# Moving one attention unit's tail tiles and six small matmul trios in a fused attention and mixture-of-experts kernel

## The chip, the cores and the metric

The kernel runs on one core of a Trainium2 chip. A core has five engines with their own instruction queues: PE (TensorE, matmuls, with PEld as its weight loads), DVE (VectorE), ACT (ScalarE), POOL (GpSimd) and SP (SyncE, used here to issue DMAs). Each engine works through its own queue in program order and waits on semaphores that other engines and DMAs raise. The metric is the device time of one execution in microseconds (us); less is better.

## The reference, cut to what matters

Three stages follow each other. The first is causal attention over 4 batches, 8 heads, 576 tokens and 64 dimensions with a decay bias from `s`; the second is a mixture-of-experts layer whose input is the attention output, the third a gated convolution layer.

```
scores = scale * q @ k.T                          # per batch and head
cum = cumsum(maximum(s, 0))
scores = where(causal, -1e9, scores + minimum(-(cum_i - cum_j), 0))
attn = softmax(scores)
x = attn @ v                                      # 576 x 64 per head
...
x = moe(x, w_gate, w_local, w1, w2)               # one expert per token
out = conv_gate(x, w_in, conv_w, w_out)
```

The change touches only the beginning of the attention stage.

## The kernel before

The attention works in 8 units of 4 heads (unit `u` is half of a batch). A unit has 14 score tiles, `(head, g)`, each a tile of 512 columns: `g` 0 and 1 are a head's own key blocks, `g` 2 is shared by two heads, and on odd heads `g` 2 and `g` 3 are the tails, the last 64 of the 576 tokens. One score tile is one step of the loop over `t` at the end of `attention`. At step `t`, PE makes the scores of tile `t` (`scores`, L482, L485, L510); ACT takes the exponentials of tile `t-1` (`weights`, L521, L526, L527); DVE forms the low half of tile `t-2` (`rest`, L538); and four steps after the last tile of a head PE multiplies with v (`values`, L554).

A unit needs work ahead of its first step. `load` brings k and q from memory (L166, issued by SP), `split_hi` on ACT (L259) and `split_lo` on DVE or POOL (L265 to L268) cut them into two f16 halves, `turn` transposes them by DMA (L277, SP), `extra` adds the decay rows (L281), and `copy` on DVE (L285) puts them in place. `stage_a` makes scores only for their row maxima, in 14 pieces (PE L382, DVE L385 and L413); `max_turn` (PE L450), `max_out` (ACT L455) and `max_row` (DMA L462, L465) bring the maxima into row 70 of the operands. `loadv` loads v of half a batch (L176, L180: twelve DMAs), and `split_v` cuts it (ACT L342 and DVE L346 for unit 0, POOL L344 to L350 for the others).

When each of these is issued is written in the table `PAR` by step number: `PAR["start"]` for unit 0 and the preparation of units 1 and 2 (negative numbers stand before step 0; within a step, in the order of the fraction), `PAR["u1"]`, `PAR["u2"]`, `PAR["u3"]` and `PAR["u"]` for the later units, relative to the first step of the unit (step 14 for unit 1). `pa` and `pn` are the first step and the number of steps of the 14 pieces, `sv` the step of `split_v`, `mx` the step of the maxima. `BEGIN` holds the order of unit 0's tiles; index 1 is used. All engines' queues follow from the order in which this code runs.

`busy(z, n)` issues `n` products of a unit matrix, 512 columns wide, into a PSUM tile that nobody reads (L368).

The pool `zps` has three PSUM tiles for scores; a score tile gives its place back when its exponentials (or, for a tile with a low half, the subtraction on DVE) are done. `mps` has one tile, which `busy` and `max_turn` share. `aps` has two for the pieces.

Of the kernel before, what the change touches and what calls it, by code (L numbers as in the profile page):

```python
# [42 lines left out]
class Keep:  # L43
# [3 lines left out]

PAR = {'u1': {'sv': -6, 'pa': -6, 'pn': 4, 'mx': -3},  # L50
 'u2': {'at': (-22, -21, -19, -18.9, -18), 'cp': (-14, -13), 'lv': -11, 'sv': -2, 'pa': -12, 'pn': 7, 'mx': -6},
 'u3': {'load': -35, 'loadq': 0, 'at': (-33, -30, -28, -27, -26.9), 'cp': (-22, -21), 'sv': -1, 'pa': -20, 'pn': 14, 'mx': -6},
 'u': {'load': -51,
# [34 lines left out]
           'hk1': -17,  # L88
           'mob': -16,
           'mrb': -15,  # L90
           'tlk': -14,
           'tlq': -13,
           'lk1': -12,
           'xt': -11,
           'T1k': -10,
           'ttk': 2.0,
           'ttq': 3.0,
           'hq1': 3.05,
           'lq1': 3.06,
           'T1q': 3.07,  # L100
           'x1': 3.08,
           'lk2': 3.09,
           'lq2': 3.095,
           'ct': 4.0,
           'pt': 4.1,
           'c2': 4.5,
           'mtt': 5.0,
           'mot': 5.1,
           'mrt': 5.2,
           'sv0': 5.4,  # L110
           'z': 6.0,
           'lv1': 6.1},
 'r': {'cut': 12, 'w1': 6, 'w2': 8, 'w3': 22},
 'm': 'faafaafaafaa'}


BEGIN = ([(0, 0), (0, 1), (1, 0), (1, 1), (0, 2), (1, 2), (1, 3)],
         [(0, 0), (0, 1), (1, 0), (1, 1), (2, 0), (2, 1), (0, 2), (1, 2), (1, 3), (3, 0), (3, 1), (2, 2), (3, 2), (3, 3)])


def attention(tc, ctx, q, k, v, s, xd, rt, hook):
# [46 lines left out]
    def loadv(b, part=None, D=Q):  # L168
        if part in (None, 0):
            U[b, "v"] = natv.tile([128, H, 4, 64], F32, name="nv")  # L170
            U[b, "vt"] = natv.tile([128, H // 2, 64], F32, name="nvt")
        w, wt = U[b, "v"], U[b, "vt"]
        h = slice(0, H) if part is None else slice(NH * part, NH * part + NH)
        for j in range(4):
            for t in range(2):
                D.dma_start(w[64 * t:64 * t + 64, h, j], v[b, h, 128 * j:128 * j + 128].rearrange("h (p t) d -> t p h d", t=2)[t])  # L176
        for e in range(2):
            for t in range(2):
                r = 64 * e + 32 * t
                D.dma_start(wt[r:r + 32, h.start // 2:h.stop // 2], v[b, h, 512:576].rearrange("(r e) (p t) d -> e t p r d", e=2, t=2)[e, t])  # L180
# [148 lines left out]
    def split_v(u):  # L329
        b, o = u // 2, u % 2 * NH  # L330
        a, t = U[b, "v"][:, o:o + NH], U[b, "vt"][:, o // 2:o // 2 + 2]
        w = U[u, "vv"] = vp.tile([128, NH, 4, 2, 65], F16, name="vv")
        wt = U[u, "vvt"] = vp.tile([128, NH // 2, 2, 65], F16, name="vvt")
        v0 = U[u, "v0"] = vp.tile([128, NH, 65], F32, name="v0")
        for x in (w, wt):
            i = (slice(None),) * (len(x.shape) - 2)
            G.memset(x[i + (0, slice(64, 65))], 1.0)
            G.memset(x[i + (1, slice(64, 65))], 0.0)
        G.memset(v0[:, :, 64:65], 1.0)
        for x, dh, dl in ((a, w[:, :, :, 0, 0:64], w[:, :, :, 1, 0:64]), (t, wt[:, :, 0, 0:64], wt[:, :, 1, 0:64])):  # L340
            if u == 0 or not PAR["h"]["vg"]:
                A.activation(dh, x, AF.Copy, scale=VS)  # L342
            else:
                G.tensor_scalar(dh, x, VS, 0.0, op0=ALU.mult, op1=ALU.add)  # L344
            if u == 0:
                V.scalar_tensor_tensor(dl, in0=x, scalar=VS, in1=dh, op0=ALU.mult, op1=ALU.subtract)  # L346
            else:
                G.tensor_scalar(x, x, VS, 0.0, op0=ALU.mult, op1=ALU.add)
                G.tensor_tensor(dl, x, dh, op=ALU.subtract)
        G.tensor_scalar(v0[:, :, 0:64], a[:, :, 0], VS if u == 0 else 1.0, 0.0, op0=ALU.mult, op1=ALU.add)  # L350
# [15 lines left out]
    def busy(z, n):  # L366
        for _ in range(n):
            PE.matmul(z.rearrange("p (x c) -> p x c", c=128), lhsT=id16, rhs=bc(id16[:, None], [128, 4, 128]), start=True, stop=True, skip_group_check=True)  # L368
# [282 lines left out]
    copy(0, "q")  # L651
    load_tail("q")
    load(1, "k")
    todo, pieces, copies = {}, {}, {6: [(1, "k")], 7: [(1, "q")]}

    def plan(t, f):
        todo.setdefault(math.floor(t), []).append((t, len(todo), f))
# [13 lines left out]
    def second_a(r):  # L671
# [12 lines left out]
        xt=extra_tail, ct=copy_tail, ldq1=lambda: load(1, "q"), lk2=lambda: load(2, "k"), lq2=lambda: load(2, "q"),  # L684
        T1k=lambda: [turn(1, e, slice(0, 1)) for e in range(2)], T1q=lambda: [turn(1, e, slice(1, 2)) for e in range(2)], x1=lambda: extra(1),
        pt=lambda: second_a(range(12, 15)), mtt=lambda: max_turn(0, None), mot=lambda: max_out(0, None), mrt=lambda: max_row(0, None),
        sv0=lambda: split_v(0), lv1=lambda: loadv(0, 1),
        z=lambda: Q.dma_start(xd[NT:NT + 128].rearrange("p (j c) -> p j c", c=256), bc(zero[:, None, 0:256], [128, 4, 256])))
    for n, t in PAR["start"].items():
        plan(t, begin_tasks[n])  # L690
# [31 lines left out]
    for t in range(N + 9):  # L722
        if t == N - 2 * PER - 6:
            early.close()
        for f in am:
            f()
        am = []
        work(t)
        at = lambda d: steps[t - d] if 0 <= t - d < N else None
        if at(0):  # L730
            scores(at(0))
        for u, i in pieces.get(t, ()):
            if i == 0:
                P[u] = stage_a(u)
            am.append(P[u][i]())
        if at(1):
            weights(at(1))
        if at(2):
            rest(at(2))
        for d, f in ((4, values), (5, norm), (6, xout)):  # L740
            y = at(d)
            if y and y[2] == (3 if y[1] % 2 else 2):
                f(y[0], y[1])
        y = at(7)
        if y and y[2] == 3 and y != (NU - 1, 1, 3):
            store(y[0], y[1] // 2)
        if at(8) == (NU - 1, 3, 3):
            rt.turn_last(U[NU - 1, "xh"], U[NU // 2 - 1, "xth"], 1, zps)
            put(NU - 1, range(1, 2))
        y = at(PAR["h"]["ps"])  # L750
        if y and y[1:] == (3, 3) and y[0] < NU - 1:
            put(y[0], range(2))
        if at(11) == (NU - 1, 1, 3):
            rt.turn_last(U[NU - 1, "xh"], None, 0, zps)
        if at(9) == (NU - 1, 1, 3):
            store(NU - 1, 0)
            put(NU - 1, range(1))
        y = at(PAR['h']['lg'])
        if y and y[1:] == (3, 3) and y[0] < NU - 1:
            rt.logits(y[0], mps.tile([128, 512], F32, name="mt"))  # L760
        y = at(PAR['h']['lg'] + PAR['h']['co'])
        if y and y[1:] == (3, 3) and y[0] < NU - 1:
            rt.collect(y[0])
        for f in tm:
            f()
        tm = []
        for n, (d, h) in enumerate(((10, 1), (12, 1), (10, 3), (12, 3), (14, 3))):
            y = at(d)
            if y and y[1:] == (h, 3) and y[0] < NU - 1 and (n < 4 or y[0] % 2):
                u = y[0]  # L770
                tm.append(rt.turn_tile(u, U[u, "xh"], U[u // 2, "xth"] if n == 4 else None, n, mps.tile([128, 512], F32, name="mt")))
        for x in copies.get(t, ()):
            copy(*x)
        hook(t)
# [803 lines left out]
```

## Time and profile before

| what | us |
|---|---|
| median of 3 runs | 713.57 |
| the 3 runs | 713.11, 713.57, 715.43 |
| the profiled execution, its own time | 710.43 |
| its span, first to last instruction | 708.7 |
| PE busy | 643.1 |
| DVE busy | 452.1 |
| ACT busy | 390.5 |
| POOL busy | 249.6 |

The profiled execution is one run with a hardware profile; its time lies 1.73 us above its span, the part of the run outside the first and the last instruction. Its mean granted TensorE clock is 0.942 of full speed. Attention fills the first 238 us; the change lies in the first 90 of them.

### The profile page before, as it was taken

The numbers are of one execution on the slowest core, as the hardware profiler recorded it, in microseconds if no ns is written. First come the engines' busy times: TensorE is split into PE (matmuls) and PEld (weight loads), VectorE is DVE, ScalarE is ACT, GpSimd is POOL, SyncE is SP. The second block draws the span as 40 slices with busy tenths as digits, with TensorE's granted clock in tenths as the row PEclk, the third lists the DMA queues.
The fourth block names the chain that finished last, engine by engine and source line by source line (L and its number), as shares of the span: only waits on it lengthen the run. The fifth ranks groups of instructions, "written<-read, shape, count | busy, mean of one in ns | idle before, by whom it ended". The sixth has DMA issues, their size and how long they took to land. (4 is left out here: it accounts for less than half of the span.)

```text
span 708.7 us, 15489 instructions
## 1 busy us (share of the span) xinstructions
PE 643.1 (91%) x5177; PEld 401.2 (57%) x5177; DVE 452.1 (64%) x859; ACT 390.5 (55%) x660; POOL 249.6 (35%) x356
## 2 busy tenths in 40 slices
PE   5668899899999566999998999999889999999997
PEld 2346778688888433444443444444367766665443
DVE  7874978988875699653885866753039985546000
ACT  5544667788788754743755563532049974645111
POOL 7456866654441059832344363333100000000000
PEclk9855989999999769999999999999999999999999
DMA  5767784756646445899999999963195000000111
GB/s 131 136 164 150 127 178 75 172 104 108 191 139 217 127 139 190 246 320 257 256 295 248 300 206 260 204 147 65 50 172 97 1 16 22 25 31 30 45 50 55
DMA packets 168828, 101.82 MB, mean 144 GB/s; under 512 B 119712, under 2 KB 147016, under 8 KB 168732
## 3 DMA queue, kind: packets, MB, share of 16 engines
q1 hardware_dynamic: 164744, 88.65, 52.2%
q0 software_dynamic: 3984, 11.99, 5.6%
q8 instruction: 47, 0.77, 0.5%
q14 instruction: 49, 0.40, 0.2%
q10 hardware_dynamic: 4, 0.00, 0.0%
HBM read 62.18 MB, written 15.31 MB: 109 GB/s over the span
## 5 line engine op out<-in xcount | busy, mean ns | idle before, releaser
L1188 PE MATMUL hp<-r,xt 128*128 x504 | 115.4, 387 | 7.9 <-ACT xt L1219 7.9
L1188 PE MATMUL yp<-r,ht 128*128 x504 | 112.2, 379 | 1.7 <-PEq L1295 1.7
L1386 PE MATMUL hp<-yt,wi 128*128 128x288 f16 x768 | 95.6, 286 | 2.5 <-DMA yt<-yd 2.5
L1434 PE MATMUL o<-wo,g 128*128 128x512 f16 x432 | 94.5, 379 | 0.0
L1188 PEld LDWEIGHTS <-xt 128*128 128x128 f16 x504 | 50.0, 99 | 69.3 <-ACT xt L1219 8.6
L1386 PEld LDWEIGHTS <-wi 128*128 128x128 f16 x768 | 75.1, 98 | 23.3 <-DMA yt<-yd 2.7
L1188 PEld LDWEIGHTS <-ht 128*128 128x128 f16 x504 | 48.5, 98 | 57.4 <-issue 1.8
L1144 DVE SCALAR_TENSOR_TENSOR r<-st,r 128x512 f32 (+3 forms) x80 | 70.7, 951 | 6.7 <-ACT r L1133 5.1
L1434 PEld LDWEIGHTS <-g 128*128 128x128 f16 x432 | 42.3, 98 | 49.5
L1133 ACT ACTIVATE r<-st 128x512 f32 (+3 forms) x84 | 57.1, 764 | 21.8 <-SPq L1181 16.8
L385 DVE TENSOR_REDUCE mx<-za 128x1 f32<-128x384 f32 (+4 forms) x97 | 57.0, 602 | 17.7 <-PE za L382 17.0
L1249 POOL DMA_INDIRECT yd<-ys,idx x21 | 23.6, 1122 | 125.6 <-DVEq L1172 77.6
L526 ACT ACTIVATE phi<-z,lnes 128x512 f16<-128x512 f32 (+1 forms) x80 | 50.6, 633 | 25.9 <-PE z L485 25.6
L482 PE MATMUL z<-k 71*128 71x128 f16 (+2 forms) x320 | 53.6, 294 | 8.5 <-ACT p L521 3.2
L538 DVE TENSOR_TENSOR plo<-z,phi 128x512 f16<-128x512 f32 (+1 forms) x80 | 48.2, 603 | 12.3 <-ACT z L527 11.7
L1403 DVE SCALAR_TENSOR_TENSOR c<-hb,cw,c 128x576 f32<-128x576 f32 x32 | 26.1, 816 | 35.3 <-ACT c L1397 35.3
L527 ACT ACTIVATE z<-z,lnes 128x512 f32<-128x512 f32 (+1 forms) x80 | 48.6, 607 | 0.0
L554 PE MATMUL o<-v,p 128*128 128x65 f32 x256 | 46.1, 293 | 0.0
L1437 ACT ACTIVATE s<-o 128x512 f32<-128x512 f32 x18 | 10.7, 597 | 63.1 <-PE o L1434 63.1
L1247 ACT ACTIVATE ys<-yp,pp 128x512 f16<-128x512 f32 x21 | 14.4, 685 | 53.5 <-PE yp L1188 32.3
L554 PE MATMUL o<-vv,phi 128*128 128x65 f16 (+1 forms) x512 | 42.7, 204 | 0.0
L554 PEld LDWEIGHTS <-phi 128*128 128x128 f16 x544 | 42.1, 110 | 0.0
(285 smaller groups left out, 1193.5 us busy)
## 6 DMA issues: line engine op xcount, KB each, us to landing
st<-in_moe_w_dram SPq DMA_DIRECT2D x8, 2048.0 KB
st<-in_moe_w_dram SPq DMA_DIRECT2D x24, 512.0 KB
out_dram<-s SPq DMA_DIRECT2D x18, 256.0 KB
st<-in_k_dram SPq DMA_DIRECT2D x16, 256.0 KB
st<-in_q_dram SPq DMA_DIRECT2D x16, 256.0 KB
xd<-xh SPq DMA_DIRECT2D x16, 256.0 KB
k<-in_moe_w_dram SPq DMA_DIRECT2D x8, 512.0 KB
s<-in_moe_w_in_dram SPq DMA_DIRECT2D x16, 256.0 KB
```

Source lines behind the costliest of these rows:

```text
L385: return lambda: V.tensor_reduce(out, z.rearrange("p (e c) -> p e c", e=m), axis=AX.X, op=ALU.max)
L482: PE.matmul(out, lhsT=ks[i], rhs=qs[i], start=first and not i, stop=False, skip_group_check=True)
L526: A.activation(hi[:, 0:n], z[:, 0:n], AF.Exp, bias=lnes, scale=1.0 / SC)
L527: A.activation(p[:, 0:n], z[:, 0:n], AF.Exp, bias=lnes, scale=1.0 / SC)
L538: (V if md == "a" else G).tensor_tensor(lo[:, 0:n], p[:, 0:n], hi[:, 0:n], op=ALU.subtract)
L554: PE.matmul(out, lhsT=w, rhs=x, start=first, stop=last, skip_group_check=True)
L1133: i = self.nc.scalar.activation(hi, src, AF.Copy, scale=self.scale[w])
L1144: i = nc.vector.scalar_tensor_tensor(lo, in0=src, scalar=sc, in1=hi, op0=ALU.mult, op1=ALU.subtract)
L1188: i = self.nc.tensor.matmul(out, lhsT=lhsT, rhs=self.rings[w][:, c, k, bass.ds(s, 1), f], **kw)
L1386: PE.matmul(st[x][:, n, 0:HN], lhsT=wi[:, c, k, m], rhs=t[:, n, a + k], start=k + a + c == 0, stop=k == 3 and a == 4)
L1403: V.scalar_tensor_tensor(c, in0=h[:, 1:S + 1], scalar=cw[:, m, 1:2], in1=c, op0=ALU.mult, op1=ALU.add)
L1434: PE.matmul(o, lhsT=g[:, a, k, 128 * i:128 * i + 128], rhs=wo[:, c, k], start=j == 0, stop=j == 23)
```

## The change

Three things change. Behind the scores of steps 1 to 6 PE gets three unit-matrix products. The two tail tiles (1,2) and (1,3) of unit 0 go from steps 7 and 8 to steps 10 and 11, and (3,0), (3,1) and (2,2) come two steps sooner each. And the table moves the work for the tails (`tlk` to `ttq`, `ct`, `pt`, `mtt`, `mot`, `mrt`) to later places, unit 1's pieces from 4 steps to 5 beginning one sooner, and v of batch 0's second half (`lv1`) from SP's queue at step 6.1 to POOL's queue ahead of step 0.

```diff
-PAR = {'u1': {'sv': -6, 'pa': -6, 'pn': 4, 'mx': -3},
+PAR = {'u1': {'sv': -5, 'pa': -7, 'pn': 5, 'mx': -3},
...
-           'mtt': 5.0,
-           'mot': 5.1,
-           'mrt': 5.2,
...
+           'mtt': 7.0,
+           'mot': 7.1,
+           'mrt': 7.2},
...
-         [(0, 0), (0, 1), (1, 0), (1, 1), (2, 0), (2, 1), (0, 2), (1, 2), (1, 3), (3, 0), (3, 1), (2, 2), (3, 2), (3, 3)])
+         [(0, 0), (0, 1), (1, 0), (1, 1), (2, 0), (2, 1), (0, 2), (3, 0), (3, 1), (2, 2), (1, 2), (1, 3), (3, 2), (3, 3)])
...
-    todo, pieces, copies = {}, {}, {6: [(1, "k")], 7: [(1, "q")]}
+    todo, pieces, copies = {}, {}, {5: [(1, "k")], 6: [(1, "q")]}
...
-        sv0=lambda: split_v(0), lv1=lambda: loadv(0, 1),
+        sv0=lambda: split_v(0), lv1=lambda: loadv(0, 1, G),
...
         if at(0):
             scores(at(0))
+            if 1 <= t <= 6:
+                busy(mps.tile([128, 512], F32, name="mt"), 3)
```

The first place is SP's queue behind the loads of unit 2 (the last load of q and the write of zeros that stand on top); `nv` and `nvt` are v and its tails, the k and q loads below them are those of unit 3 and the k of unit 4, and `k_693` (`k_717` in the new program) is what unit 2's transposes write.

```order
 L166 DMA st_112<-in_q_dram 128x4x128 x2
 L688 DMA xd<-zero 512x1x256
-L176 DMA nv<-in_v_dram 64x4x64 x8
-L180 DMA nvt<-in_v_dram 32x2x64 x4
 L166 DMA st_112<-in_k_dram 128x4x128 x2
 L166 DMA st_112<-in_q_dram 128x4x128 x2
 L166 DMA st_111<-in_k_dram 128x4x128 x2
-L277 DMA_TRANSPOSE k_693<-h 128x32x64 x2
+L277 DMA_TRANSPOSE k_717<-h 128x32x64 x2
```

The twelve DMAs of v leave SP here; the loads of unit 3 come directly behind the zeros. They stand in POOL's queue behind the first twelve, ahead of all of POOL's work for steps 0 to 6.

The second place is ACT's queue from the exponentials of step 3 (`L526`, `L527`) to those of step 8; `L455` and `L465` bring out unit 0's tail maxima, the `L259` that write `h` split k and then q of unit 2, and the `L259` that writes `st_111` splits k of unit 3. Before:

```order
L526 ACTIVATE phi<-z,lnes 128x512
L527 ACTIVATE z<-z,lnes 128x512
L455 ACTIVATE mr<-mt 2x128
L465 DMA t_141<-mr 1x2x128
L342 ACTIVATE vv<-nv 128x16x64
L342 ACTIVATE vvt<-nvt 128x2x64
L521 ACTIVATE p_578<-z,lnes 128x512
L259 ACTIVATE h<-st_111 128x16x64
```

Now, from the split of unit 2's k on:

```order
L259 ACTIVATE h<-st_111 128x16x64
L526 ACTIVATE phi<-z,lnes 128x512
L527 ACTIVATE z<-z,lnes 128x512
L259 ACTIVATE h<-st_112 128x16x64
L455 ACTIVATE mr<-mt 2x128
L465 DMA t_141<-mr 1x2x128
L526 ACTIVATE phi<-z,lnes 128x512
L527 ACTIVATE z<-z,lnes 128x512
L521 ACTIVATE p_696<-z,lnes 128x512
L259 ACTIVATE st_111<-st_112 128x16x64
```

The tail maxima went from ahead of step 4's exponentials to behind the split of unit 2's q, ahead of step 6's.

The third place is DVE's queue from the two copies of unit 0's tails (`L327`) to the second copy of unit 1's operands (`L285`), as it stands now; before, the `L385` and `L413` rows stood directly behind `L327`, and the two `L285` behind them.

```order
L327 COPY t_141<-t_142 64x4x512 x2
L346 SCALAR_TENSOR_TENSOR vv<-nv,vv 128x16x64
L346 SCALAR_TENSOR_TENSOR vvt<-nvt,vvt 128x2x64
L538 TENSOR_TENSOR plo<-z,phi 128x512
L285 COPY k_139<-k_424 64x2x1024
L385 TENSOR_REDUCE mx<-za 128x2
L413 ISA za,mx<-za,zero,mx 128x512
L413 ISA mx 128x1
L413 ISA za,mx<-za,zero,mx 128x512
L413 ISA mx 128x1
L285 COPY k_139<-k_424 64x2x1024
```

The tail maxima went behind v's split, one subtraction and the first copy of unit 1.

## Rows read from the trace of the kernel before

**Rows 1.** The page's slices: the granted clock, 40 equal parts of the span

```profile
PEclk9855989999999769999999999999999999999999
```

**Rows 2.** Busy time by stretch of the span: engines, granted clock, DMA share, GB/s

```profile
core 0: us, PE busy (x) PEld busy (x) DVE busy (x) ACT busy (x) POOL busy (x), PEclk, DMA share, GB/s
24.60:30.40 5.80, 3.56 (x45) 2.81 (x45) 5.01 (x6) 4.28 (x9) 1.98 (x8) 0.99 0.26 41
30.40:47.10 16.70, 8.79 (x60) 4.99 (x58) 11.55 (x17) 9.53 (x15) 4.08 (x3) 0.50 0.80 163
47.10:71.30 24.20, 21.56 (x157) 16.27 (x158) 13.02 (x29) 8.62 (x18) 17.88 (x26) 0.50 0.70 143
71.30:88.80 17.50, 14.93 (x201) 12.28 (x199) 16.09 (x36) 11.71 (x23) 15.76 (x38) 0.99 0.69 128
88.80:95.10 6.30, 5.77 (x35) 3.97 (x33) 3.46 (x9) 3.71 (x7) 5.61 (x18) 0.50 0.82 156
142.00:238.00 96.00, 90.97 (x1421) 79.29 (x1419) 73.76 (x201) 76.14 (x145) 35.85 (x55) 1.00 0.59 157
```

**Rows 3.** PE's timeline: start, length, instruction, idle time before it and its releaser

```profile
12.45 1.03 PE L368 MATMUL mt<-id 128*128 128x512 f16 x4
...
34.80 0.32 PE L382 MATMUL za<-t 70*64 70x64 f16 x4 [1.94 <-DVE t L327]
...
41.86 1.01 PE L482 MATMUL z<-k 71*128 71x256 f16 x4 [2.60 <-ACT p L521]
...
47.11 0.61 PE L382 MATMUL za<-k 70*128 70x128 f16 x4 [1.33 <-DVE k L285]
...
70.01 1.06 PE L482 MATMUL z<-k 71*128 71x512 f16 x2
```

**Rows 4.** ACT's timeline around its waits

```profile
38.12 0.27 ACT L455 ACTIVATE mr<-mt 2x128 f16<-2x128 f32 x1 [3.99 <-PE mt L450]
38.46 1.19 ACTq L465 DMA_DIRECT2D t<-mr  x1
...
44.59 1.06 ACT L259 ACTIVATE h<-st 128x1024 f16<-128x1024 f32 x1 [0.60 <-DMA st<-in_q_dram]
...
53.52 1.06 ACT L259 ACTIVATE st<-st 128x1024 f16<-128x1024 f32 x1 [5.59 <-DMA st<-in_k_dram]
54.48 0.35 ACT L526 ACTIVATE phi<-z,lnes 128x128 f16<-128x128 f32 x1
```

**Rows 5.** SP's queue, DMA issues in order of time

```profile
27.93 8.09 SPq L277 DMA_TRANSPOSE k<-st  x4
...
38.84 1.14 SPq L166 DMA_DIRECT2D st<-in_q_dram  x2
...
40.71 5.36 SPq L176 DMA_DIRECT2D nv<-in_v_dram  x8
...
48.18 2.28 SPq L166 DMA_DIRECT2D st<-in_k_dram  x2
...
53.41 7.69 SPq L277 DMA_TRANSPOSE k<-h  x2
61.14 2.30 SPq L281 DMA_DIRECT2D k<-ex  x2
```

**Rows 6.** POOL's timeline: the first load of v, and the end of its later idle time

```profile
16.38 4.94 POOL L176 DMA_DIRECT2D nv<-in_v_dram  x8
...
22.18 1.60 POOL L180 DMA_DIRECT2D nvt<-in_v_dram  x3 [0.32 <-DMA nv<-in_v_dram]
...
42.94 1.04 POOL L267 TENSOR_SCALAR st<-st 128x1024 f32<-128x1024 f32 x1 [16.28 <-ACT h L259]
```

**Rows 7.** PE's products with v alone (L554), four heads' stretches by start and end

```profile
57.12:59.94 2.82, 2.82 (x26) 2.82 (x26) 0.50 0.80 165
65.22:69.69 4.47, 4.47 (x41) 4.40 (x41) 0.50 0.37 105
76.15:78.52 2.37, 2.37 (x41) 2.35 (x41) 1.00 0.89 124
```

More of the change, by code (lines that the diff above doesn't have):

```diff
@@ L90 @@
            'mrb': -15,
[L91 to L106, printed above, removed]
-           'mtt': 5.0,
-           'mot': 5.1,
-           'mrt': 5.2,
-           'sv0': 5.4,
-           'z': 6.0,
-           'lv1': 6.1},
+           'lk1': -14,
+           'xt': -13,
+           'T1k': -12,
+           'lv1': -11,
+           'tlk': 1.05,
+           'tlq': 1.06,
+           'hq1': 2.05,
+           'lq1': 2.06,
+           'T1q': 2.07,
+           'x1': 2.08,
+           'lk2': 2.09,
+           'lq2': 2.095,
+           'ttk': 3.0,
+           'ttq': 4.0,
+           'ct': 5.0,
+           'sv0': 5.4,
+           'c2': 5.5,
+           'pt': 6.1,
+           'z': 6.2,
+           'mtt': 7.0,
+           'mot': 7.1,
+           'mrt': 7.2},
  'r': {'cut': 12, 'w1': 6, 'w2': 8, 'w3': 22},
```

## The prediction

> **What bounds the kernel now.** I read the page's slices first, then the stretches, then the timelines of single engines in the slow part, then SP's queue. The slices show TensorE's granted clock near full speed except in three places: slices 2 to 4, slice 5, and slices 13 to 14, where the next stage begins [rows 1]. By stretches: full clock to 30.40, half of it (1.2 GHz instead of 2.4) from 30.40 to 71.30, full again to 88.80, half to 95.10 [rows 2]. From 142 to 238 PE is busy 90.97 of 96.00 at full clock, so in the later units PE paces attention, and a unit that begins sooner ends sooner by as much. What can be gained lies in the first 95 us.
>
> There two things take turns. From 30.40 to 47.10 PE is busy only 8.79 of 16.70 [rows 2]; its waits have many releasers: DVE's copies of the tails, ACT's exponentials, DVE's copies of unit 1 [rows 3]. From 47.10 to 71.30 it is busy 21.56 of 24.20 at half clock: PE itself is the bound, and only because of the clock [rows 2]. From 71.30 to 88.80 PE runs at full speed and DVE is the fullest engine, 16.09 of 17.50.
>
> ACT is what the early steps wait for. It stood 3.99 for unit 0's tail maxima (38.12), 0.60 for unit 2's q (44.59), and 5.59 for unit 3's k (53.52), with step 8's exponentials and all later ones queued behind [rows 4]. Unit 3's k came late because SP issued twelve DMAs of v ahead of it: they take SP from 40.71 to 48.18, 7.47 us [rows 5].
>
> **The change, part by part.** *v's load leaves SP.* Unit 3's loads move 7.47 forward in SP's queue, directly behind the zeros. Landed 5.34 after the issue as before (48.18 to 53.52), k would be there at about 46. POOL takes the twelve DMAs instead. Its first twelve took 16.38 to 23.78, 7.4 us, with a wait for a landing among the last [rows 6], so I put the new ones at 24 to 32, and to 38 if each waits for landings. POOL was idle for 16.28 until 42.94 and has only small work for step 10 in between, so this costs nothing; without that cover it would cost up to 7.4.
>
> *ACT's gate.* ACT's split of unit 2's q at step 7 waited for its load, issued at 38.84 [rows 4, 5]. In front of that load in SP's queue nothing changes: the transposes of unit 1 still begin when the maxima and decay rows are issued and take 8.09. So I leave the gate at 44.59, though PE will reach it with steps 4 to 6 done much earlier. What is won ahead of the gate is lost in it: this is why I give the 2.60 and 1.94 waits of [rows 3] no credit. Behind the gate ACT did 8.93 - 5.59 = 3.34 us of work up to unit 3's split [rows 4]. Now the tail maxima (0.27) and their DMA issue (1.19) stand there too: 4.80, so unit 3's split starts at 49.4 instead of 53.52. Its data is there by then. **4.1 us sooner** for ACT from step 8 on.
>
> *PE behind the gate.* Before, unit 1's pieces began at 47.11 and its first scores at 70.01 [rows 3]: 22.90, of which 21.56 - 1.29 = 20.27 busy and 2.6 idle [rows 2]. Now the work in between holds the products with v of heads 0 and 2 in place of heads 0 and 1, 2.82 for an even head against 4.47 [rows 7]; the other steps that change sides cancel to about 0.1. That leaves 18.7. The pieces' copies are a step earlier, but the row maxima queue on DVE behind subtractions that wait for ACT, so I let all of it begin by ACT's 4.1 sooner, at 43.0. At half clock and with the same idle time unit 1 begins at 43.0 + 18.7 + 2.6 = 64.3, 5.7 sooner; the 1.65 of head 1 is still owed: **a gain of 4.0**. At full clock the products go by 2.37 to 4.47, a factor of 0.53 [rows 7]: 9.9 + 2.6, so PE could be through at 55.5. Then SP is next: unit 2's transposes and decay rows, 7.69 + 2.30 [rows 5], stand ahead of the DMA of unit 1's maxima. They began at 53.41 and can begin at 45.9 to 50, after POOL's splits; the maxima go out at 56 to 60 and unit 1 starts near 58 to 62. That is 8 to 12 sooner with 0.9 owed: a gain of 7 to 11.
>
> *The unit products.* Eighteen, at most 1.03 / 4 = 0.26 each at full clock [rows 3]: 4.6; at half clock 8.7. PE is idle 2.24 + 7.91 = 10.1 from 24.60 to 47.10 [rows 2], before ACT's gate, so they are hidden; without that cover they cost those 4.6 to 8.7. What they buy is clock. In 24.60 to 30.40 PE was busy 3.56 of 5.80 and the clock fell right after. With two or three trios there it is busy for nearly all of it, so I expect full clock past 30.40. But there are waits left that no trio fills: PE's second tail tile waits for a row maximum that now stands on DVE behind v's split and unit 1's first copy, and the maxima's turn waits for two more; I put PE mostly idle from 36 to 42. I therefore expect half clock again from about 40 for most of the work behind the gate, and take most of the half-clock value.
>
> *DVE and the tails.* The same instructions in another order; the tail scores are three steps later, so their maxima have more time. Nothing gained or lost alone.
>
> The sum: 4.0 at half clock, 7 to 11 at full; nearest to the first, with a little full clock in it: 5.0. Against the profiled execution's own 710.43 that is 705.4. The median of the runs is 3.14 above that execution, so for it I forecast 708.6. About 0.3% (2.1 us) is what a measurement of this kernel can tell from no change.
>
> **The rivals.** *The clock holds.* The trios and the closer order keep PE at full speed through unit 0. For it: the trios close the 24.60 to 30.40 stretch. Against: the waits from 36 to 42. Time: 7 to 11 less, 702.6 to 706.6.
>
> *The transfers collide.* v's transfers move from 40 to 48 to the time of unit 1's transposes (27.93 to 36.02), where the DMA engines are already busy 0.80 from 30.40 to 47.10 [rows 2]. Then the transposes, and with them unit 2's loads and the gate at 44.59, come later by x, and the gain shrinks by x. An x of 5 leaves nothing; it needs the twelve transfers to hold up SP by two thirds of their old 7.47 in its queue. Against: from 24.60 to 30.40 the share is only 0.26, and most of v is issued there. Time: 711.5 to 715.7. Here a rule bears: the Trainium skill, DMA: Bandwidth & Descriptors, section Issuing engines are not separate DMA queues, says that DMAs started by any engine interleave on the same 16 DMA engines, and another issuer saves only the issue time. No row of before shows v's transfers beside transposes; by this rule alone the change takes SP's 7.47 of issue away and no transfer, and the time would lie between this rival and the forecast.
>
> *Slower: the clock comes back later.* Before, it came back at 71.3, after PE had run nearly without a gap. With unit 1 beginning sooner and the products of head 1 pushed into it, PE could meet DVE's fullest stretch still at half speed. Price: the 14.93 busy of 71.30 to 88.80 [rows 2] would be 28.2, or 10.7 longer. It decides from the point where half of that stretch runs at half speed, which eats the 5.0. In full it gives 5.7 more: 719.3. Against: the dense part that ended at 71.3 is still there, only sooner.
>
> **How the numbers follow.** The forecast, gain 3 to 7: 0.60. The clock holds, gain over 7: 0.14. The transfers collide, within about 2 of before: 0.14. The clock comes back later: 0.12. The first two are faster, 0.74; the third is the same, with a little of its edges, 0.14; the last is slower, 0.12. The range takes in the full-clock case down to 702.6 and the colliding transfers up to about 713.5; the forecast's own is 706.6 to 710.6.
>
> **What would show it.** In the profile after: no `nv` DMA in SP's queue near 40, twelve more on POOL from 24; ACT's split of unit 3's k without its 5.59 wait; ACT's split of unit 2's q still at 43 to 46, after a wait that is now longer; the granted clock at full past 30.4 and at half again before 47; unit 1's first scores at 62 to 66 instead of 70.01; from there on the old distances. The prediction is wrong if the gate moves (the transposes of unit 1 slower or faster), if the clock never falls, or if the stretch behind unit 1's start grows by what was won ahead of it.

## The result and the profile after

The changed kernel took 718.50 us in the median of six runs (717.16 to 721.07), the kernel before 714.67 in its six; the ratio, from which disturbed runs are left out, is 1.0110 with a 95% interval of 1.0068 to 1.0153. Timed once more, the medians were 719.44 and 711.35 and the ratio 1.0122 (1.0060 to 1.0184). So it is some 1.1% slower by both ratios (the first two medians alone stand 0.5% apart), where 708.6 us, 0.7% faster, was forecast. The profiled execution took 717.16, its span is 715.1.

In the opening the profile looks as forecast. Slices of the granted clock, then the stretches of [rows 2] in the changed kernel:

```profile
PEclk9965879999999678999999999999989999999999
```

```profile
24.60:30.40 5.80, 3.97 (x36) 2.51 (x36) 4.89 (x6) 4.57 (x8) 5.65 (x10) 1.00 0.57 132
30.40:47.10 16.70, 13.93 (x93) 8.79 (x93) 11.34 (x20) 7.62 (x13) 6.79 (x12) 0.72 0.89 197
47.10:71.30 24.20, 20.96 (x193) 16.59 (x190) 13.62 (x30) 12.83 (x24) 20.46 (x27) 0.56 0.64 113
71.30:88.80 17.50, 14.14 (x168) 10.75 (x166) 16.27 (x35) 9.26 (x20) 15.98 (x51) 0.91 0.80 152
88.80:95.10 6.30, 5.43 (x34) 4.35 (x33) 2.58 (x4) 4.01 (x7) 3.41 (x5) 0.50 0.63 97
142.00:238.00 96.00, 91.57 (x1423) 79.84 (x1420) 73.57 (x201) 75.35 (x144) 37.49 (x56) 0.99 0.61 157
```

From 30.40 to 47.10 PE is busy 13.93 us where it was 8.79, at a clock of 0.72 for 0.50 [rows 2]. Unit 1's transposes take about what they took, and unit 3's loads leave SP without v in front of them (SP's queue):

```profile
27.84 7.77 SPq L277 DMA_TRANSPOSE k<-st  x4
...
39.87 0.65 SPq L688 DMA_DIRECT2D xd<-zero  x1
40.57 2.41 SPq L166 DMA_DIRECT2D st<-in_k_dram  x2
```

ACT's timeline answers to [rows 4]. Its lines with `mr<-mt` (L455) copy a unit's row maxima and so mark where each unit stands: here the tails of unit 0, then units 1, 2, 3 and 7.

```profile
41.68 1.06 ACT L259 ACTIVATE h<-st 128x1024 f16<-128x1024 f32 x1 [4.10 <-DMA st<-in_k_dram]
...
44.67 1.06 ACT L259 ACTIVATE h<-st 128x1024 f16<-128x1024 f32 x1 [0.81 <-DMA st<-in_q_dram]
45.63 0.25 ACT L455 ACTIVATE mr<-mt 2x128 f16<-2x128 f32 x1
...
48.92 1.06 ACT L259 ACTIVATE st<-st 128x1024 f16<-128x1024 f32 x1
49.87 0.69 ACT L526 ACTIVATE phi<-z,lnes 128x512 f16<-128x512 f32 x1
...
61.78 0.27 ACT L455 ACTIVATE mr<-mt 18x128 f16<-18x128 f32 x1 [6.56 <-PE mt L450]
...
88.50 0.27 ACT L455 ACTIVATE mr<-mt 18x128 f16<-18x128 f32 x1 [3.94 <-PE mt L450]
...
99.31 0.69 ACT L526 ACTIVATE phi<-z,lnes 128x512 f16<-128x512 f32 x1 [5.46 <-PE z L485]
...
116.54 0.27 ACT L455 ACTIVATE mr<-mt 18x128 f16<-18x128 f32 x1 [1.92 <-PE mt L450]
...
206.63 0.27 ACT L455 ACTIVATE mr<-mt 18x128 f16<-18x128 f32 x1 [0.26 <-PE mt L450]
```

The same marks in the kernel before:

```profile
64.47 0.27 ACT L455 ACTIVATE mr<-mt 18x128 f16<-18x128 f32 x1 [7.68 <-PE mt L450]
...
91.17 0.27 ACT L455 ACTIVATE mr<-mt 18x128 f16<-18x128 f32 x1 [5.20 <-PE mt L450]
...
98.09 0.69 ACT L526 ACTIVATE phi<-z,lnes 128x512 f16<-128x512 f32 x1 [3.02 <-PE z L485]
...
115.32 0.27 ACT L455 ACTIVATE mr<-mt 18x128 f16<-18x128 f32 x1 [1.92 <-PE mt L450]
...
205.42 0.27 ACT L455 ACTIVATE mr<-mt 18x128 f16<-18x128 f32 x1 [0.26 <-PE mt L450]
```

Unit 1 is 2.69 us ahead, unit 2 still 2.67, and unit 3 is 1.22 behind; from there the distance stays to unit 7 (1.21). So 3.9 us vanish between 88 and 117 us, and PE's timeline shows the place:

```profile
65.65 1.04 PE L482 MATMUL z<-k 71*128 71x512 f16 x2
...
90.08 0.63 PE L916 MATMUL mt<-unit,xh 128*128 128x128 f16 x4
91.58 0.59 PE L916 MATMUL mt<-unit,xh 128*128 128x128 f16 x4 [0.87 <-ACT xT L917]
91.96 1.06 PE L482 MATMUL z<-k 71*128 71x512 f16 x2
...
93.56 1.06 PE L554 MATMUL o<-v,p 128*128 128x65 f32 x4
...
98.00 1.06 PE L482 MATMUL z<-k 71*128 71x128 f16 x6
```

L916 are the four products that turn a finished tile of unit 0 for the routing (`turn_tile`). Two such groups now stand side by side in step 23, and the second waits 0.87 us for the tile `mt`, of which `mps` has one: ACT empties it (L917) only behind two tiles' exponentials. In the kernel before one group stands there (the same line, L914, as that program is two lines shorter):

```profile
92.75 0.63 PE L914 MATMUL mt<-unit,xh 128*128 128x128 f16 x4
93.18 1.06 PE L482 MATMUL z<-k 71*128 71x512 f16 x2
...
94.78 0.80 PE L554 MATMUL o<-v,p 128*128 128x65 f32 x4
...
97.33 0.62 PE L482 MATMUL z<-k 71*128 71x128 f16 x6
```

So PE is 2.67 us ahead at the first group (90.08 for 92.75) and 1.22 ahead at step 24's scores behind the second (91.96 for 93.18). The products with v behind them take 4.44 us at half clock (93.56 to 98.00) where they took 2.55 (94.78 to 97.33), and that turns the lead into 0.67 behind. Half clock lasts from 85.6 to 99.2 us here and from 88.4 to 95.2 before (in slices of 0.2 us; the expectations below read it coarser, as 12.8 and 6.3). It begins ahead of the collision.

That is 1.2 us at unit 7. The span is 6.4 longer: from unit 7's maxima to its end it took 508.5 us (715.1 - 206.63) and 503.3 before (708.7 - 205.42). So there are two losses to explain, one inside attention and one behind it. Of the second a part may belong to the executions that were profiled: the one of the kernel before took 710.43, 4.2 us under the median of its six, the one of the changed kernel 1.3 under its own.

### The profile page after: what moved, and what is told of

Its sections match the earlier page's. It is cut to its first block, busy times and chain, and to the rows that moved or that the text cites. A ratio compares the mean times of both kernels' runs of the same rounds, so it can differ in the third digit from the quotient of the medians.

```text
span 715.1 us, 15530 instructions
## 1 busy us (share of the span) xinstructions
PE 649.2 (91%) x5195; PEld 406.3 (57%) x5195; DVE 451.2 (63%) x859; ACT 391.4 (55%) x660; POOL 256.2 (36%) x368
## 5 line engine op out<-in xcount | busy, mean ns | idle before, releaser
L1190 PE MATMUL hp<-r,xt 128*128 x504 | 115.1, 386 | 9.3 <-ACT xt L1221 8.1
L1190 PE MATMUL yp<-r,ht 128*128 x504 | 112.2, 379 | 1.7 <-PEq L1297 1.7
L1388 PE MATMUL hp<-yt,wi 128*128 128x288 f16 x768 | 98.0, 291 | 4.9 <-DMA yt<-yd 4.9
L1190 PEld LDWEIGHTS <-xt 128*128 128x128 f16 x504 | 50.0, 99 | 70.8 <-ACT xt L1221 9.2
L1190 PEld LDWEIGHTS <-ht 128*128 128x128 f16 x504 | 48.5, 98 | 57.4 <-issue 1.8
L1146 DVE SCALAR_TENSOR_TENSOR r<-st,r 128x512 f32 (+3 forms) x80 | 71.2, 954 | 5.5 <-ACT r L1135 4.4
L385 DVE TENSOR_REDUCE mx<-za 128x1 f32<-128x384 f32 (+4 forms) x97 | 57.0, 602 | 18.0 <-PE za L382 17.0
L526 ACT ACTIVATE phi<-z,lnes 128x512 f16<-128x512 f32 (+1 forms) x80 | 50.6, 632 | 30.4 <-PE z L485 27.5
L1405 DVE SCALAR_TENSOR_TENSOR c<-hb,cw,c 128x576 f32<-128x576 f32 x32 | 26.1, 814 | 37.6 <-ACT c L1399 37.6
L527 ACT ACTIVATE z<-z,lnes 128x512 f32<-128x512 f32 (+1 forms) x80 | 48.5, 606 | 0.0
L554 PE MATMUL o<-v,p 128*128 128x65 f32 x256 | 47.4, 298 | 0.0
L554 PE MATMUL o<-vv,phi 128*128 128x65 f16 (+1 forms) x512 | 43.2, 206 | 0.0
L1393 ACT ACTIVATE hb<-hp 128x576 f32<-128x576 f32 x32 | 20.8, 650 | 40.7 <-PE hp L1388 40.2
```

The lines of the kernel that those rows point to most:

```text
L385: return lambda: V.tensor_reduce(out, z.rearrange("p (e c) -> p e c", e=m), axis=AX.X, op=ALU.max)
L526: A.activation(hi[:, 0:n], z[:, 0:n], AF.Exp, bias=lnes, scale=1.0 / SC)
L527: A.activation(p[:, 0:n], z[:, 0:n], AF.Exp, bias=lnes, scale=1.0 / SC)
L554: PE.matmul(out, lhsT=w, rhs=x, start=first, stop=last, skip_group_check=True)
L1146: i = nc.vector.scalar_tensor_tensor(lo, in0=src, scalar=sc, in1=hi, op0=ALU.mult, op1=ALU.subtract)
L1190: i = self.nc.tensor.matmul(out, lhsT=lhsT, rhs=self.rings[w][:, c, k, bass.ds(s, 1), f], **kw)
```

## The experiments

Eighteen runs followed, of fourteen new kernels; 7, 8, 17 and 18 repeat a kernel. For each: the ratio to the kernel before with its interval, the half-clock stretches between 80 and 102 us, the copies of unit 3's and unit 7's maxima, and the span from there to its end ("rest"). These last four are of one profiled execution, the ratio of 6 to 12 timed runs. "Off" is how far the profiled execution's time lies from the median of its kernel's runs (for 7, of the runs of the kernel before beside it).

| kernel | ratio | half clock, us | unit 3 | unit 7 | rest | off |
|---|---|---|---|---|---|---|
| before | 1 | 88.4-95.2 | 115.32 | 205.42 | 503.3 | -4.2 |
| before again (7) | 1 | 89.2-92.6 | 113.66 | 203.72 | 504.1 | -1.9 |
| changed | 1.0110 (1.0068-1.0153) | 85.6-99.2 | 116.54 | 206.63 | 508.5 | -1.3 |
| changed again (8) | 1.0122 (1.0060-1.0184) | 84.4-98.2 | 115.51 | 205.60 | 506.4 | -5.3 |
| 1 trios alone | 0.9980 (0.9945-1.0015) | 90.6-100.8 | 118.67 | 210.30 | 502.3 | 0.0 |
| 2 no trios | 1.0041 (1.0019-1.0063) | 91.0-94.4 | 112.43 | 203.99 | 506.7 | -3.4 |
| 3 v on POOL alone | 0.9991 (0.9965-1.0017) | 87.4-94.2 | 114.40 | 204.50 | 510.2 | +4.5 |
| 4 turnings apart | 0.9994 (0.9973-1.0015) | 84.6-91.4 | 111.86 | 201.96 | 509.2 | +0.3 |
| 5 apart, no trios | 1.0019 (0.9977-1.0062) | 90.4-97.2 | 115.44 | 206.93 | 507.9 | +3.6 |
| 6 apart, trios also at 20-22 | 0.9991 (0.9952-1.0030) | none | 109.56 | 198.08 | 510.0 | +0.4 |
| 9 as 6, v on SP | 0.9933 (0.9896-0.9969) | none | 113.46 | 201.95 | 501.9 | -3.5 |
| 10 apart, trios at 20-22 only | 0.9960 (0.9926-0.9994) | none | 109.35 | 199.40 | 508.1 | +0.3 |
| 11 before, trios at 20-22 | 0.9963 (0.9931-0.9996) | none | 113.04 | 203.11 | 504.7 | +0.8 |
| 12 changed, trios also at 20-22 | 1.0074 (1.0036-1.0113) | 90.8-94.2 | 112.41 | 202.28 | 505.7 | -6.2 |
| 13 as 10, v on SP | 0.9986 (0.9961-1.0012) | none | 113.23 | 201.74 | 511.6 | +5.7 |
| 14 changed, v on SP | 1.0046 (1.0024-1.0068) | 82.6-92.8 | 115.23 | 203.74 | 502.1 | -4.3 |
| 15 as 11, v on POOL | 1.0015 (0.9982-1.0048) | none | 112.25 | 200.76 | 511.7 | +1.2 |
| 16 as 11, v read by both | 1.0001 (0.9972-1.0029) | none | 113.79 | 202.11 | 506.1 | +0.1 |
| 17 as 9, again | 0.9950 (0.9920-0.9979) | none | 113.16 | 204.59 | 503.1 | +1.4 |
| 18 as 6, again | 0.9973 (0.9940-1.0007) | none | 109.38 | 200.81 | 509.5 | +1.3 |

Single executions of one kernel lie some 9 us apart (before, 34 runs of one comparison: 707.52 to 716.12), so the ratios carry the verdicts, and the profiles say where. The profiles of 12, 14 and 2 are the fastest of their kernels' runs and those of 3 and 13 the slowest; a rest has to be read with that. The four kernels that were profiled twice repeat their rest within 2.1 us. A ratio is against runs of the kernel before on the same chip, whose median differs from chip to chip (710.79 to 714.67).

### One part at a time: 1 to 4

1 adds to the kernel before:

```diff
+            if 1 <= t <= 6:
+                busy(mps.tile([128, 512], F32, name="mt"), 3)
```

> The kernel before with the six trios of unit products and nothing else of the change. Three theories stand for the 3.8 us that the change lost. A: the opening is won (unit 1's first scores 4.4 us sooner) and the loss is made at 90 to 99 us, by the four turning products that wait there 0.87 us for the tile `mt` and by the half-clock stretch that grew from 6.3 to 12.8 us. B: the trios are the loss: what they cover in the opening is small, and 18 products of 0.25 to 0.5 us each move later work. C: v's second load on POOL is the loss, by another order of landings. A expects 711 to 716 us here (no change by more than 0.3%, unit 1's first scores between 67 and 71 us); B expects 717 to 720; C expects no change, 713 to 716.

2 takes the same two lines out of the changed kernel.

> The changed kernel without the trios. A: the collision of the two turnings at step 23 stays, so the loss stays in part: 716 to 720 us, with unit 1's first scores at 65 to 68 us and unit 3's maxima within 1 us of 116.5. B: the loss goes with the trios, 709 to 714 us. C: the loss stays, 717 to 720.

3 moves `lv1` in the kernel before:

```diff
+           'lv1': -9.5,
...
-           'lv1': 6.1},
...
-lv1=lambda: loadv(0, 1),
+lv1=lambda: loadv(0, 1, G),
```

> The kernel before with one edit of the change: v's second load leaves SP and is issued on POOL ahead of the first step. A: SP's 7.47 us are won at the q split and little else moves, since the table's order is the old one: 711 to 714.5 us. B: the same. C: the loss of the change is here, 716 to 720 us.

4 edits the changed kernel where the turnings are issued:

```diff
-            y = at(d)
+            y = at(d - 1 - n if h == 1 and t < 24 else d)
             if y and y[1:] == (h, 3) and y[0] < NU - 1 and (n < 4 or y[0] % 2):
```

> The changed kernel with one edit: the two turnings of unit 0's tile (1, 3) go to steps 20 and 21, so that step 23 has only one tile's turning. A expects the 0.87 us wait ahead of step 24's scores to be gone, the half-clock stretch from 86 us to end by 96 to 97 us and unit 3's maxima at 114.5 to 115.5 us instead of 116.54: 714 to 717 us. If the wait goes and the stretch still lasts to 98 us, the collision is no cause of the stretch: 717 to 718.5 us. B and C expect no change from 718.5 us.

Trios alone (1: 714.39 us) and v on POOL alone (3: 712.26) change nothing that can be told from no change: B and C fall, as single causes. With the turnings apart (4: 712.91) the changed kernel is level with the one before, better than A's 714 to 717, and the half-clock stretch ends at 91.4, well ahead of A's 96 to 97. So the turnings at their new steps, two of them at step 23, are needed for the 1.1%. No run has them as late without two at one step, so that it is the meeting and not the lateness rests on the wait of 0.87 us. Marks of 4 on ACT, and what PE waits for in its experts:

```profile
61.06 0.27 ACT L455 ACTIVATE mr<-mt 18x128 f16<-18x128 f32 x1 [6.56 <-PE mt L450]
...
87.91 0.27 ACT L455 ACTIVATE mr<-mt 18x128 f16<-18x128 f32 x1 [4.04 <-PE mt L450]
...
111.86 0.27 ACT L455 ACTIVATE mr<-mt 18x128 f16<-18x128 f32 x1 [1.92 <-PE mt L450]
...
201.96 0.27 ACT L455 ACTIVATE mr<-mt 18x128 f16<-18x128 f32 x1 [0.26 <-PE mt L450]
```

```profile
341.60 5.34 PE L1190 MATMUL hp<-r,xt 128*128 x24 [2.74 <-ACTq L1174]
...
388.55 6.96 PE L1190 MATMUL hp<-r,xt 128*128 x24 [3.56 <-ACT xt L1221]
```

Unit 3 is 4.68 ahead of the changed kernel and 3.46 ahead of before, as is unit 7 (1.8 ahead of the second profile of before, 7): with the collision away, the opening's gain reaches the end of attention. It doesn't reach the end of the kernel: L1190 waits 2.74 + 3.56 for the experts' weights and rows, where the kernel before waited once (L1188 there):

```profile
388.60 7.03 PE L1188 MATMUL hp<-r,xt 128*128 x24 [2.84 <-ACT xt L1219]
```

The two waits are 3.46 longer than that one, just what unit 7 had won; the last expert block's copy stands at 505.35 us against 505.47. Behind that copy 4 takes 2.6 us more again (205.8 for 203.2).

Without trios (2: 716.19) the collision stays and the loss shrinks to 0.41%, at the edge of what A allowed; unit 3's maxima, which A put within 1 us of 116.5, came at 112.43, with a half-clock stretch of 3.4 us: the trios are part of the loss where there is a collision, and of none where there is not (4 against 5, 1 against before).

### The clock and the collision: 5 to 8 and 10 to 12

5 is 4 without the trios; 6 is 4 with:

```diff
-            if 1 <= t <= 6:
+            if 1 <= t <= 6 or 20 <= t <= 22:
```

> The changed kernel with the turnings of tile (1, 3) at steps 20 and 21 and without the trios. If the collision at step 23 is what the change lost, and the trios neither gain nor cost, this is as the run with the turnings apart and the trios: 711 to 714.5 us, unit 1's maxima copied at 60.5 to 62 us, unit 7's at 201 to 203.5 us (205.42 before, 206.63 after). If the trios hold something up by themselves, unit 7's maxima come over 1.5 us sooner than 201.96 and the time is 708 to 711; if their clock is worth something, it is 714 to 717.

> The changed kernel with the turnings apart and the same trios also behind the scores of steps 20 to 22, where PE waits for DVE's maxima before the clock falls at about 86 us. If that idle time is what lets the clock fall, the half-clock stretch between 85 and 97 us goes or shrinks under 4 us, unit 3's maxima are copied at 108 to 110.5 us (111.86 with the turnings apart) and unit 7's at 198 to 200.5; the time falls by less, to 709 to 712.5, if the later stages absorb a gain. If the trios only stand in the way, the stretch stays 7 us or longer and unit 7's maxima come at 202 to 204.

7 and 8 are the two kernels unchanged.

> The kernel before, once more, for a second profile. If its first profile (710.43, under the median of its runs) was a favourable one in the stages after attention, unit 7's maxima come again at 205.4 (within 0.7 us) and the last expert block's copy comes 1.5 us or more after 505.47; the time is 711 to 716. If the later stages repeat, that copy is within 0.7 us of 505.47, and the 2.6 to 3.5 us that the changed kernels lose there belong to the change.

> The changed kernel once more, against the kernel before on the chip of this call. If the loss is the change's, 716 to 720 us and 0.4 to 1.1% over before; the turning products wait 0.8 to 1.9 us for `mt` again, and the half-clock stretch that begins at about 86 us lasts over 8 us. If it was that run's alone, within 0.3% of before.

10 is 6 with `if 20 <= t <= 22:` alone, 11 the kernel before with those two lines, 12 the changed kernel with the edit of 6.

> The run with the turnings apart, with trios at steps 20 to 22 alone and none in the opening. If the opening's trios gain nothing, unit 1's maxima are copied at 61.0 to 62.0 us, unit 7's at 197 to 199.5 us and the time is 707 to 712 us, as with both. If their higher clock ahead of unit 1 is worth something, unit 1's maxima come over 1 us later than 61.65 and unit 7's over 199.5.

> The kernel before with nothing but three unit products behind the scores of steps 20 to 22. If the idle time there lets the clock fall, the half-clock stretch of 3.5 to 6.3 us goes and unit 7's maxima come at 199.5 to 202.5 us instead of 203.7 to 205.4; if the later stages pass it on, 708 to 711 us (0.3 to 0.6% under before), and if they absorb it, no change by more than 0.3%.

> The changed kernel with its collision of two turnings at step 23, and with trios also at steps 20 to 22. If the clock is what the change lost at 85 to 98 us, and the wait for `mt` only its 0.9 to 1.9 us, unit 7's maxima come at 198.5 to 201 us and the time is 709 to 714. If the collision is the loss at any clock (it holds up the values behind it), the clock falls behind the wait all the same, unit 7's maxima come at 204 to 206.6 and the time is 715 to 720.

The stretch from 85.00 to 99.00, columns as in [rows 2]: before, changed, 12, 6.

```profile
85.00:99.00 14.00, 12.00 (x127) 9.20 (x126) 9.44 (x23) 5.59 (x11) 9.86 (x37) 0.76 0.81 143
```

```profile
85.00:99.00 14.00, 12.19 (x88) 9.62 (x88) 6.16 (x15) 4.31 (x8) 6.62 (x20) 0.52 0.79 148
```

```profile
85.00:99.00 14.00, 11.79 (x148) 10.51 (x148) 8.00 (x19) 8.00 (x17) 6.26 (x15) 0.88 0.78 143
```

```profile
85.00:99.00 14.00, 13.05 (x195) 11.14 (x196) 10.73 (x27) 10.26 (x20) 9.10 (x21) 1.00 0.84 162
```

The changed kernel is busier there than before (12.19 for 12.00) and does less: 88 records for 127, at 0.52 of full clock. In 6 the nine products behind steps 20 to 22 stand where PE had waited for DVE's maxima of unit 2, and the clock does not fall at all; the same holds for 9 to 11, 13 and 15 to 18, every run with these trios and no collision. In 12 the collision breaks it even so. PE of 12:

```profile
89.43 0.38 PE L916 MATMUL mt<-unit,xh 128*128 128x128 f16 x4 [1.89 <-ACT xT L917]
```

At full speed PE is through with the first turning sooner, so the wait is 1.89 instead of 0.87, and the clock falls at 90.8, behind it, until 94.2. Unit 3 comes 2.85 us later than in 6 (112.41 for 109.56). The time stays 0.74% over before: of my two readings, the second, that the collision is the loss at any clock, had the time right (715 to 720; 716.26), while unit 7's maxima (202.28) lie between the two. They are of an execution of 710.07 us, the fastest of its twelve.

The distance from the copy of unit 2's maxima to that of unit 3's says more, set beside the time that the clock was at half between these two marks:

| kernel | unit 2 to unit 3, us | at half clock, us |
|---|---|---|
| 6, 9 to 11, 13, 15 to 18: late trios, no collision | 22.2 | 0 |
| 7 (before) | 23.3 | 2.3 |
| 4 | 24.0 | 3.6 |
| 3 | 24.1 | 3.8 |
| before | 24.2 | 4.0 |
| 5 | 25.4 | 6.8 |
| 1 | 26.2 | 8.4 |
| 14, with the collision | 24.4 | 2.1 |
| 2 and 12, with the collision | 26.1 | 3.4 |
| changed and 8, with the collision | 28.0 | 10.8 and 10.6 |

Without the collision the distance is 22.2 plus 0.48 to 0.49 for each us at half clock, in all fifteen profiles. By that the changed kernel pays 5.2 of its 28.0 to the clock, where before paid 1.9, and 0.6 to the collision itself: most of the 3.9 us lost here goes through the longer stretch at half clock. Where PE comes to the collision at full speed (2 and 12) it costs 2.2 by itself and 1.7 through the clock behind it. So both readings of 12 were half right. That the stretch lasts longer because of the collision rests on 4, which lacks it and whose stretch is 6.8 us in its one profile, for 13.6 in both profiles of the changed kernel; 14 has the collision and a stretch that ended ahead of it.

11 is the opposite case: nothing of the change but the trios, moved to where PE waits. Its half-clock stretch is gone and it is 0.37% faster than before (708.71 us), with an interval just clear of 1; unit 7 came at 203.11, not the 199.5 to 202.5 expected. 6 had everything that was expected of it (198.08, 709.75 us) and still passed on next to nothing: 0.09%.

The opening's own trios gained nothing at unit 1: its maxima are copied at 61.78 and 60.71 us in the changed kernel's two profiles, and at 61.45 and 60.88 in 2 and 10, which lack them. 5 missed its expectation: unit 7 came at 206.93, not 201 to 203.5. Its clock rose only at 73.4 us (67.6 in 4) and the half-clock stretch was again 6.8; that is one execution, and its ratio cannot be told from that of 4.

7 met neither of its expectations, as unit 7 was 1.7 sooner, with a half-clock stretch of 3.4, and the time 709.48; but it repeated the stages behind attention (last expert block's copy at 503.12, which is 299.4 us behind unit 7's maxima, for 300.1 in the first profile). Both executions lie under the median of their runs. So a part of the 2 to 5 us that the changed kernel's profiles need more behind unit 7 may be theirs, and the rest of it still has to be explained.

### v's place, and what lies behind attention: 9 and 13 to 18

9 is 6 with v's second load back on SP, behind unit 0's last small transfers; 13 is 10, and 14 the changed kernel, with the same edit:

```diff
-           'lv1': -11,
...
-           'mrt': 7.2},
+           'mrt': 7.2,
+           'lv1': 7.3},
...
-lv1=lambda: loadv(0, 1, G),
+lv1=lambda: loadv(0, 1),
```

15 is 11 with the edit of 3. 16 is 11 with v's second half read by POOL at step -9.5 as well as by SP at 6.1. 17 and 18 are 9 and 6 once more, on one chip.

> The run with the turnings apart and trios also at 20 to 22, but with v's second load back on SP's queue, behind the last of unit 0's small transfers. From unit 7's maxima to the end both profiles of the kernel before took 503.3 and 504.1 us of the span, the changed kernels and the others with v on POOL 506.4 to 510.2. If v's place on POOL makes that difference, it is 503 to 505 here and the time 703 to 707 us. If the later stages only give back what attention wins, it is 507 to 511 for unit 7's maxima at 197 to 200 us, and the time is 708 to 712.

> Unit 0's tails further back as in the change, turnings apart, trios at steps 20 to 22 alone, v's second load on SP behind unit 0's small transfers. If v on POOL lengthens the stages behind attention (from unit 7's maxima to the end 501.9 to 504.7 us in the five profiles with it on SP, 505.7 to 510.2 in the nine with it on POOL) this takes 501.5 to 505 there, and is 0.5 to 1% under before: 704 to 709 us. If those stages only give back what attention wins, 506 to 510 there and 708 to 712 us.

> The changed kernel with one edit: v's second load back on SP's queue, behind unit 0's small transfers; collision and trios as in the change. If v on POOL costs 3 to 5 us in the later stages, these take 501.5 to 505 us and the time is within 0.5% of before, 711 to 715, where the change was 1.1 to 1.2% over. If the collision alone is the loss, 716 to 720.

> The kernel before with trios at steps 20 to 22 and with v's second load on POOL ahead of the first step. The same with v on SP took 504.7 us from unit 7's maxima to the end and was 0.37% under before. If v on POOL is what lengthens these stages: 506 to 510 there, and the time level with before or over it. If not: 503 to 505.5, and again 0.2 to 0.6% under before.

> The kernel before with trios at steps 20 to 22 and v's second half read twice: by POOL ahead of the first step, and by SP where it was, into the same tile. If POOL's queue being used for these 12 transfers is what lengthens the later stages, they take 506 to 510 us here too; if it is SP's queue having 12 transfers fewer, 502 to 505; if neither matters, 503 to 505.5 in both this run and the one with v on POOL alone.

> The run with the turnings apart, trios at steps 1 to 6 and 20 to 22 and v on SP, once more, on the same chip as its twin with v on POOL. If v's queue is worth 0.5 to 0.7%, this is 0.4 to 0.8% under before and its twin within 0.3% of before; from unit 7's maxima to the end 501.5 to 505 us against 506 to 511. If not, the two are within 0.3% of each other.

> The twin with v on POOL: within 0.3% of before and 506 to 511 us from unit 7's maxima to the end if v's queue matters; 0.3 to 0.7% under before, like its twin, if it does not. The half-clock stretch at 85 to 98 us is gone in both, and unit 7's maxima come before 202.5 us.

The rest is 501.9 to 504.7 us in seven of the eight profiles with v on SP and 505.7 to 511.7 in the eleven with v on POOL. Among those whose unit 7 comes between 203.5 and 205.6, so that giving back a gain cannot be the difference, it is 502.1, 503.1, 503.3 and 504.1 on SP, and 506.4, 506.7 and 510.2 on POOL. The times lean the same way in four of six pairs, SP first: 1.0046 in 14 against 1.0110 and 1.0122 in the changed kernel, 0.9933 in 9 against 0.9991 in 6, 0.9963 in 11 against 1.0015 in 15, and 0.9950 in 17 against 0.9973 in 18. They don't in 13 against 10 (0.9986, 0.9960), nor in before against 3 (0.9991). Not all of 14's gain is made behind attention: its unit 7 is 2.9 and 1.9 us ahead of the changed kernel's two profiles. The half-clock stretch ended ahead of the collision's wait (0.87 again, until 93.87), and the clock did not fall near 140 us as it did in both of those. All these edits move v's place in time along with its queue. In the pair on one chip 17 took 708.08 and 18 711.03 in the median, though 18 ended attention 3.78 us sooner in its profile. The last marks of 17 and 18, a wait in 18's experts, and SP's queue in 17 and then in 18:

```profile
204.59 0.27 ACT L455 ACTIVATE mr<-mt 18x128 f16<-18x128 f32 x1 [0.26 <-PE mt L450]
```

```profile
200.81 0.27 ACT L455 ACTIVATE mr<-mt 18x128 f16<-18x128 f32 x1 [0.26 <-PE mt L450]
```

```profile
342.48 7.03 PE L1190 MATMUL hp<-r,xt 128*128 x24 [4.18 <-ACTq L1174]
```

```profile
46.05 5.32 SPq L176 DMA_DIRECT2D nv<-in_v_dram  x8
...
53.84 6.78 SPq L277 DMA_TRANSPOSE k<-h  x2
```

```profile
48.83 5.55 SPq L277 DMA_TRANSPOSE k<-h  x2
```

In 17 v's loads hold SP's queue, and unit 2's transposes begin 5.0 us later than in 18; the clock rises at 74.4 us instead of 67.2, and unit 2's maxima come at 90.97 instead of 87.18. That the first is the cause of the others is not shown. 9 had the rest that v's queue would have it (501.9), with unit 7 later than expected (201.95 for 197 to 200); its profiled execution, 705.49, lay in the 703 to 707 us expected and its median, 709.03, did not.

But it is not settled. 13 has v on SP and a rest of 511.6, with one wait of 4.52 us at 424.6 in its experts, and its time is no better than that of 10; the profile is the slowest of its twelve runs. 3 has v on POOL and is level with before. 16, which uses both queues, lies between (506.1), but its clock was at half from 212.6 to 219.4 us, in attention's last unit, and its first expert product came 59.0 us behind unit 7's maxima, for 56.6 in 11. From that product to the end it took 447.1 us, as the seven on SP did (445.2 to 448.1; 449.3 to 455.5 in the eleven on POOL). By its expectation that speaks for SP's queue being twelve transfers short rather than for POOL's being used; it is one execution, and its ratio (1.0001) does not bear it out. The intervals of 17 and 18 overlap. No row shows which later transfer v's queue holds up. Part of the longer rest appears as waits of L1190 in the experts, at 322 to 425 us and up to 4.18 us, at various of their blocks; but the longest in the changed kernel's first profile is 1.93 us, for 2.84 before.

The kernel of 9 and 17 has the lowest ratios of the study, 0.5 to 0.7% under the kernel before, with intervals clear of it both times.

## Why the prediction was wrong

- **v's load leaves SP: right** about SP. Unit 3's k went out at 40.57 instead of 48.18. What it called free ("this costs nothing") may be paid in a second place, which it did not consider: 14 against the changed kernel gives 0.6 to 0.8% for v's place, 9 against 6 and 15 against 11 0.5 to 0.6%, 17 against 18 some 0.2 (ratios) to 0.4% (medians), 10 against 13 and 3 nothing. Here the rule cited from the Trainium skill, DMA: Bandwidth & Descriptors, section Issuing engines are not separate DMA queues, would have v's issuer matter for issue time alone; the lean of these runs is against that, without deciding it, as v's time of issue moved with its issuer.
- **ACT's gate: right.** It stood at 44.67 (44.59 before), and step 8's exponentials began at 49.87 instead of 54.48: 4.6 sooner, 4.1 forecast. Both the longer wait (4.10, though for k) and the absence of the 5.59 were as said.
- **PE behind the gate: right, with a smaller size.** Unit 1's first scores came at 65.65, 4.36 sooner instead of 5.7; with 1.65 owed for head 1 that leaves 2.7, which is what unit 2 shows (2.67). Unit 1's maxima, ahead of those products, were 2.69 sooner. Forecast were 4.0 at half clock and 5.0 in the sum.
- **The unit products: hidden, and worth nothing.** The clock held until 41.2, but for 3.4 us, as forecast ("half clock again from about 40"). Unit 1 was no sooner for it.
- **The step that failed is "from there on the old distances".** Unit 2 stood 2.67 ahead and unit 3 1.22 behind, as it took 28.0 us from one to the other instead of 24.2, 3.3 of the 3.9 more by the clock. The change moved unit 0's tile (1,3) from step 8 to step 11, and with it, three steps each, the turnings that hang on it at fixed distances: from steps 18 and 20 to 21 and 23. Tile (3,3) stayed, and its first turning is at 23 too. Of the tile `mt` I had said that `busy` and `max_turn` share it; the turnings use it as well. I priced the work that the table moves, and "the other steps that change sides cancel"; what follows a tile by counting steps I did not follow, and so the second stretch at half clock was priced at nothing. Turnings apart (4) give unit 7 at 201.96, 3.46 ahead of before (1.8 ahead of its second profile; 5.0 was forecast), and the loss of the changed kernel is gone from the time (0.9994).
- **The transfers did not collide.** Unit 1's transposes took 7.77 us (8.09 before), with v's second twelve DMAs issued on POOL from 23.27 to 30.55, and the gate stayed. **The clock did not hold:** it fell again at 41.2.
- **The slower rival had the size and the wrong place.** It put half speed behind unit 1's start (719.3 us). The clock came back sooner there, at 68.6 instead of 71.2; it fell again at 85.6, and the second stretch at half speed doubled to 13.6 us.
- **A step that was not even written failed too:** that the end of attention, moved, moves the end of the kernel. 4, 6 and 18 end attention 3.5, 7.3 and 4.6 us before the kernel before and are 0.06, 0.09 and 0.27% faster, within their intervals. In 4 the two waits in the experts take all of it back; the DMA share there is 1.04 to 1.11 from 300 to 395 us already in the kernel before, but that the transfers pace this stage is argued from that and not shown.
- **A misread place.** Counted as "slices 2 to 4" are, the other two low places of [rows 1] are slice 6 and slices 14 and 15. Nothing in the sum hangs on it.

What stays open: why v's place matters up to 300 us later, if it does; and how the 1.1% divides, since taking out the collision, the trios, or v from POOL each gives half of it back or more (1.2, 0.7 and 0.6 points), more in sum than there is.

## What to carry to other kernels

When a tile is moved in an order of steps, list everything that follows it by a fixed distance, and ask for each resource with one buffer whether two of them now meet. A filler for the clock belongs where the engine waits just ahead of dense work, which may be elsewhere than the waits of the stretch that one is changing: nine products at steps 20 to 22 took a half-clock stretch away (11, 0.37%), and eighteen in the opening changed nothing that could be told (1). And read a gain at several marks up to the end, since a later stage can take it back; and ask of each profile how far its execution lies from the median.

## What the runs showed of the hardware

A wait of 1.89 us on TensorE was followed by a fall of the clock to 1.2 GHz, 1.4 us after its end in 12 and 1.6 in 2, with PE at work in between; without that wait the clock stayed at 2.4 GHz there in all nine runs that had the late trios and no collision. Being busy was not the same as being fast: over 85 to 99 us PE was busy 12.19 of 14 us at a clock of 0.52 and 12.00 at 0.76. From unit 2's maxima to unit 3's, each us at half clock made the way 0.48 to 0.49 us longer (0 to 8.4 us of it, fifteen profiles). And the same program on the same chip varied by 1.2% (707.52 to 716.12 us), more than most of the effects that were looked for.
